# Prologue of a long-convolution kernel: position blocks loaded and multiplied half by half, decay read as a laid-out constant

## The chip, the cores and the metric

The kernel runs on one core of a Trainium2 chip. The metric is the device time of one execution in microseconds. Three executions of the kernel before gave 2279.33, 2279.97 and 2280.75 us; their median, 2279.97 us, is the time before. A further execution was profiled: it took 2278.88 us, of which the profile's span, from the first to the last instruction, covers 2277.1 us.

A core has a matrix engine (TensorE, PE in the profile; its weight loads are shown apart as PEld), a vector engine (VectorE, DVE), a scalar engine (ScalarE, ACT), a general engine (GpSimd, POOL) and an engine that mostly issues transfers (SyncE, SP). Each works through its own instructions in order. Transfers are issued from the queues of SP, ACT and POOL and run on 16 shared DMA engines. On-chip memory has 128 partitions; products of TensorE land in a separate accumulator memory, PSUM.

## The reference

All arrays are 32-bit floats. The first part is a convolution along the sequence whose filter is made by a small network and damped by an exponential window; the second part is a feed-forward layer on its result.

```python
# x, v: (4, 12544, 128); pos_emb: (12544, 64); w1: (64, 64); w2: (64, 128)
h_mlp = np.maximum(pos_emb @ w1, 0.0) @ w2
window = np.exp(-0.01 * np.arange(S))[:, None]
h_filt = h_mlp * window
u = x * v
Uf, Hf = np.fft.rfft(u, n=2 * S, axis=1), np.fft.rfft(h_filt, n=2 * S, axis=0)
y = np.fft.irfft(Uf * Hf[None], n=2 * S, axis=1)[:, :S, :]
x = (x * y).reshape(B * S, D)
# moe weights w1, w2, w3: (128, 768); w_out: (768, 128)
out = np.maximum(np.maximum(x @ w1, x @ w2), x @ w3) @ w_out
```

The window falls below what a 32-bit float can hold after 128 x 82 = 10496 positions, so only these 10496 rows of `pos_emb` are used.

## The kernel before, in words

A position is written as n x 128 + p, with a block number n below 82 (`NH`) and a place p below 128. The Fourier transform of the sequence is done as a first product over n with the table `f1` (or `f1h` for the filter), and a second product over p with tables that hold the rest. The work runs in stages: a prologue (to about 112 us in the profile), a stage that multiplies the spectra of the first batch and of the filter, and then the long part, in which the feed-forward products of one batch run beside the convolution of the next. The order of instructions on every engine is that of the code: it is written by hand, and no scheduler moves them. Only the waits between engines, and the tiles' buffers, are put in by the framework.

The change lies in the prologue, which does two things side by side.

The filter. `posT`, the 64 features by position, is loaded into `pos`, which borrows the memory of `specH`. The 82 blocks are split into two halves of 41 (`HH`): half h = 0 lies in partitions 0 to 63, half h = 1 in partitions 64 to 127. Each half comes in four pieces (`cuts`), 64 partitions each, issued in turn from SP and ACT (line 303). `mlp_in(i)` (line 334) multiplies 16 places p of both halves by `w1`: for every place and half, a matmul with 64 rows of contraction, 41 stationary columns (the blocks) and 64 moving columns. Its 32 matmuls go into one of two PSUM tiles, `pm0` and `pm1`, in turn. The output of half h for odd or even place r goes to partitions from 64 * (h ^ r), so both halves share a tile: partitions 0 to 40 and 64 to 104. `mlp_out(i)` (line 346) takes the positive part and multiplies it by the decay `winr` in one VectorE instruction for each r, over 105 partitions and 512 columns, and writes it to `hs`, which borrows the memory of `spec`. There are 8 such rounds. The 32-matmul blocks are counted as 64 in the profile, since each 32-bit matmul is recorded twice. After the last, the loop `for f in range(0, FO, 4)` (line 949) calls `quad` (line 899), 16 matmuls and a ScalarE copy each, with `f1h`.

The decay. `winr` must hold the window by block in partitions, with the places of each parity in falling order. The kernel before loads two pieces of `window` from HBM into `win`, turns them on TensorE (`window_turn`, line 317), copies them on ScalarE into `winT`, and turns them back with a permuted identity, `back` (`window_back`, line 324). The tiles `win`, `winT` and `back` are lent from the pool in which the data loads `ut` live. The partitions 41 to 63 of the `pm` tiles, which no matmul writes, are zeroed by two memsets of partitions 32 to 63 (line 291).

The data. The sequence is cut into units of 16 channels. `u_load` (line 362) issues two transfers per unit from SP, `u_mul` (line 372) multiplies `x` and `v` on VectorE, `turn2` (line 890) transposes two units on TensorE (8 transposes and a ScalarE copy), and `early(u)` (line 908) does a `quad` with the data, its result put partly aside. Units 0 to 3 go through this between the rounds of `mlp_in`. Ahead of it all `warm_up` (line 309) issues 25 rounds of products of zeros, of four matmul records each.

`some(n)` issues VectorE instructions that convert the feed-forward weights from 64-bit; it begins with the loop over `f`.

Of the kernel before, what the change touches and what calls it, by code (L numbers as in the profile page):

```python
# [10 lines left out]
FP32 = mybir.dt.float32  # L11
# [5 lines left out]
P = 128  # L17
# [9 lines left out]
NH = 82  # L27
HH = NH // 2
# [63 lines left out]
def kernel(  # L92
# [15 lines left out]
    nc = tc.nc  # L108
    NG, _, _, B, NB = x.shape
    FO, S = posT.shape  # L110
# [19 lines left out]
    f1h_d = nc.inline_tensor(f1h_t, name="f1h_const").ap()  # L130
# [2 lines left out]
    wq_d = nc.inline_tensor(wq_t, name="wq_const").ap()  # L133
    sign = np.where(np.arange(N1) < NK, 1, -1).astype(np.float32)[:, None]
    sign_d = nc.inline_tensor(sign.copy(), name="sign_const").ap()
    order = 127 - (2 * np.arange(64)[None, :] + np.arange(2)[:, None]).ravel()
    back_d = nc.inline_tensor(np.eye(P, dtype=np.float32)[:, order].copy(), name="back_const").ap()
    eye_d = nc.inline_tensor(np.eye(P, dtype=np.float32), name="eye_const").ap()

    w_sb = [None] + [const.tile([D, DFF], FP32, name=f"w_sb{i}") for i in (1, 2)]  # L140
# [59 lines left out]
    def scratch(name, bufs):  # L200
        return sml.tile([P, 2 * HF], I32, tag=name, name=name, bufs=bufs)[:]

    def load_raw(i, h, eng):
        r = scratch("raw", 2)
        if i < 3:
            src = (moe_w1, moe_w2, moe_w3)[i].bitcast(I32).rearrange("(g c) f -> c g f", c=GC)
            for c in range(GC):
                eng.dma_start(r[c * NG:(c + 1) * NG],
                                  src[c][:, h * 2 * HF:(h + 1) * 2 * HF])
        else:  # L210
            src = moe_w_out.bitcast(I32).rearrange("(c p) d -> p c d", p=P)
            eng.dma_start(r.rearrange("p (c d) -> p c d", c=NF // 2),
                              src[:, h * NF // 2:(h + 1) * NF // 2, :])
        return r

    def convert(r, i, h):
# [35 lines left out]
    inp = ctx.enter_context(tc.tile_pool(name="inp", bufs=3))  # L252
# [3 lines left out]
    eye = raw0.tile([P, P], FP32, name="eye")  # L256
# [7 lines left out]
    fps = mps.enter_context(tc.tile_pool(name="fps0", bufs=2, space=PSUM))  # L264
# [5 lines left out]
    posv = pos.rearrange("f (n p) -> f p n", p=P)  # L270
    hs = spec[0:64 + HH].rearrange("p k r d -> p (k r d)")[:, 0:FO * P].rearrange(
        "n (f r t) -> n f r t", r=2, t=64)
    w1_sb = sml.tile([P, FO], FP32, name="w1_sb")
    w2_in = sml.tile([P, D], FP32, name="w2_in")
    w2x = pin.tile([P, D], FP32, name="w2x")

    def lent(n, name):
        return inp.tile([P, 4, NB], FP32, tag="u0", name=name)[:].rearrange(
            "p g n -> p (g n)")[:, 0:n]

    win = lent(P, "win")[0:64 + HH]
    winT = lent(2 * (64 + HH), "winT").rearrange("p (r n) -> p r n", r=2)
    winr = sml.tile([64 + HH, 2, 64], FP32, name="winr")
    back = lent(P, "back").rearrange("p (r t) -> p r t", r=2)
    f1h = sml.tile([64 + HH, 2, 2 * N1], FP32, name="f1h")
    warm = sml.tile([P, 256], FP32, name="warm")
    nc.vector.memset(warm[:], 0.0)
    nc.vector.memset(win, 0.0)
    pms = [fps.tile([P, 1024], FP32, name=f"pm{i}", bufs=1) for i in range(2)]
    for pm in pms:  # L290
        nc.vector.memset(pm[32:64], 0.0)
    for h in range(2):
        nc.gpsimd.dma_start(
            win[64 * h:64 * h + HH],
            window[0, h * HH * P:(h + 1) * HH * P].rearrange("(n p) -> n p", p=P))
    nc.gpsimd.dma_start(eye[:], eye_d)
    nc.gpsimd.dma_start(back.rearrange("p r t -> p (r t)"), back_d)
    for h in range(2):
        (nc.scalar if h else nc.sync).dma_start(w1_sb[64 * h:64 * h + 64], w1[:, :])
    cuts = (0, 11, 21, 31, HH)  # L300
    for j, (lo_, hi_) in enumerate(zip(cuts, cuts[1:])):
        for h in range(2):
            (nc.scalar if (h + j) % 2 else nc.sync).dma_start(
                pos[64 * h:64 * h + 64, lo_ * P:hi_ * P],
                posT[:, (h * HH + lo_) * P:(h * HH + hi_) * P])
    for r in range(2):
        nc.scalar.copy(winT[:, r, 0:64], warm[:, 0:64])

    def warm_up(n):

        ps = fps.tile([P, 1024], FP32, tag="cv", name="pw")
        for _ in range(n):
            halves_mm(ps[:, 0:256], warm[:, 0:P], warm[:], True, True)

    pw = fps.tile([P, 1024], FP32, tag="cv", name="pw")

    def window_turn():
        nc.tensor.transpose(pw[:, 0:64 + HH], win, eye[0:64 + HH, 0:64 + HH])
        for r in range(2):
            for h in range(2):  # L320
                c = 64 * (h ^ r)
                nc.scalar.copy(winT[:, r, c:c + HH], pw[:, 64 * h:64 * h + HH])

    def window_back():
        for r in range(2):
            nc.tensor.matmul(pw[0:64 + HH, 512 + 64 * r:576 + 64 * r], winT[:, r], back[:, r],
                             start=(r == 0), stop=True, skip_group_check=True)
        nc.scalar.copy(winr[:].rearrange("n r t -> n (r t)"), pw[0:64 + HH, 512:512 + P])

    def w2_order():  # L330
        nc.scalar.copy(w2x[:].rearrange("f (c g) -> f c g", c=GC),
                       w2_in[:].rearrange("f (g c) -> f c g", c=GC))

    def mlp_in(i):

        ps = pms[i % 2]
        for q in range(8):
            for r in range(2):
                for h in range(2):
                    c = 64 * (h ^ r)  # L340
                    nc.tensor.matmul(
                        ps[c:c + HH, 512 * r + q * FO:512 * r + (q + 1) * FO],
                        posv[64 * h:64 * h + 64, P - 1 - 2 * (8 * i + q) - r, :],
                        w1_sb[64 * h:64 * h + 64], start=(q == 0), stop=True,
                        skip_group_check=True)
    def mlp_out(i):
        v = pms[i % 2][0:64 + HH].rearrange("n (r t f) -> n r f t", r=2, t=8)
        for r in range(2):
            nc.vector.scalar_tensor_tensor(
                out=hs[:, :, r, 8 * i:8 * i + 8], in0=v[:, r], scalar=0.0,  # L350
                in1=winr[:, r, None, 8 * i:8 * i + 8].to_broadcast([64 + HH, FO, 8]),
                op0=ALU.max, op1=ALU.mult)

    NU = NG
# [7 lines left out]
    def u_load(b, u):  # L362
        c, g0 = divmod(u, NG // 4)
        ts = []
        for src in (xr, vr):
            t = pools(b, u).tile([P, 4, NB], FP32, tag=f"u{len(ts)}", name="ut")
            nc.sync.dma_start(
                t[:], src[4 * g0:4 * g0 + 4, :, c, b, :].rearrange("g p n -> p g n"))
            ts.append(t)
        us[u] = ts  # L370
# [519 lines left out]
    def turn2(u):  # L890

        t = utp.tile([NB, 8, 2, 64], FP32, tag="uT", name="uT")
        ps = fps.tile([P, 1024], FP32, tag="cv", name="pst")
        for v in range(2):
            turn(u + v, ps[:, 512 * v:512 * v + 512])
        nc.scalar.copy(t[:], ps[0:NB, :].rearrange("n (s t r) -> n s r t", s=8, r=2))
        uts[u] = t
# [10 lines left out]
    def early(u):  # L908
        t, v = uts[u - u % 2], 4 * (u % 2)
        quad([t[:, v + i] for i in range(4)], (f1, f1), aside[u],  # L910
             spec[:, NS:, :, 4 * u:4 * u + 4])

    warm_up(22)
    window_turn()
    warm_up(3)
    nc.scalar.dma_start(f1q[:], f1_d)
    for u in range(4):
        u_load(0, u)
    raws.append(load_raw(*jobs[0], nc.sync))
    for u in range(4, 6):  # L920
        u_load(0, u)
    raws.append(load_raw(*jobs[1], nc.sync))
    for i in range(9):
        if i in (4, 7):
            turn2(2 * (i // 7))
            for u in range(6 + 2 * (i // 7), 8 + 2 * (i // 7)):
                u_load(0, u)
        if i in (5, 6):
            early(i - 5)
        if i < 8:  # L930
            mlp_in(i)
        if i >= 7:
            early(i - 5)
        if i == 0:
            window_back()
            nc.scalar.dma_start(f1h[:], f1h_d)
            nc.scalar.dma_start(w2_in[0:FO], w2[:, :])
            nc.scalar.dma_start(w2_in[FO:P], w2[:, :])
        else:
            mlp_out(i - 1)  # L940
        if i in (3, 5):
            for u in range(i - 3, i - 1):
                u_mul(u)
    for u in (0, 2):
        uts.pop(u)
# [2 lines left out]
    fps = fin.enter_context(tc.tile_pool(name="fps", bufs=4, space=PSUM))  # L948
    for f in range(0, FO, 4):
        quad([hs[:, f + i] for i in range(4)], (f1h[:, 0], f1h[:, 1]), specH[:, :, :, f:f + 4])  # L950
        u, k = divmod(f // 4, 4)
# [12 lines left out]
    for u in range(4, NU, 2):  # L964
        t = uts.pop(u)
# [201 lines left out]
    for n, (b, i) in enumerate(tiles[:LAST]):  # L1167
# [9 lines left out]
        for f in range(NF):  # L1177
# [9 lines left out]
            h = up((b, i), f)  # L1187
# [42 lines left out]
    for i in range(0, NT, 2):  # L1230
        h = {}
        X, Y = banks if i % 4 == 0 else banks[::-1]
        for j, (name, f) in enumerate(ORDER):
            n = int(name[1]) - 1
# [5 lines left out]
            if step > 2 and weights:  # L1240
                out, a1, a2 = weights.pop(0)
# [57 lines left out]
```

## Time and profile before

| what | value |
|---|---|
| median of three executions | 2279.97 us (2279.33 to 2280.75) |
| the profiled execution | 2278.88 us |
| its span | 2277.1 us |
| TensorE busy | 2257.1 us, 99% of the span |
| VectorE, ScalarE, GpSimd busy | 69%, 52%, 39% |
| first product of positions on TensorE | at 16.08 us |
| first `mlp_out` on VectorE | at 18.87 us |
| quads with `f1h` start | at 39.34 us |

A line of the page's fifth part, or of an answer about groups, gives the line of the kernel, engine, operation, what is written from what, the shape, and the count; then the busy time, the mean length of one in ns, and the idle time before. A line of a timeline gives start, duration, engine, line and operation, with equal neighbours merged (x4: four of them); the bracket names the idle time before it and what ended that. The chain that ended last is followed back from the last instruction of the span to what each step waited for. The answers by stretch give for each engine the busy time and the count of instructions, and at the end the granted clock of TensorE, the busy share of the transfer engines and GB/s.

### The profile page before, as it was taken

The page shows a single profiled execution, that of the slowest core. Times are in us where ns is not written, and L with a number is a line of the kernel's source. Part 1 is how long each engine was busy: PE and PEld are TensorE (multiplying, and loading weights), DVE is VectorE, ACT ScalarE, POOL GpSimd, SP SyncE. Part 2 cuts the span into 40 slices and gives each one's busy share as a digit, 9 for nine tenths or more (in the row PEclk, how much of TensorE's full clock was granted, in tenths as well). Part 3 has the DMA queues.
Part 4 walks back from the last instruction along what each step waited for, and adds up shares of the span by engine and source line. Part 5 has one row for each costly group of instructions (what it writes and reads, how often), then busy time and mean ns, then how long its engine had stood idle before and what let it go on. Part 6 is the DMA issues. An engine that isn't in the chain of part 4 may idle for free.

```text
span 2277.1 us, 68484 instructions
## 1 busy us (share of the span) xinstructions
PE 2257.1 (99%) x27855; PEld 1376.3 (60%) x27855; DVE 1560.9 (69%) x2854; ACT 1174.9 (52%) x2129; POOL 877.6 (39%) x1089
## 2 busy tenths in 40 slices
PE   9999999999999999999999999999999999999998
PEld 7899866655555556655555556655555546666665
DVE  5589967677777757667878756658878754544443
ACT  3688844466666534456666534456666522222222
POOL 1045433323333334323333333423333326666666
PEclk9999999999999999999999999999999999999999
DMA  8778989699989689889999789979999732222221
GB/s 193 179 242 278 297 186 182 135 221 246 243 221 242 165 176 183 163 189 246 245 237 239 194 166 181 166 182 252 235 235 240 197 81 56 56 71 64 60 56 22
DMA packets 473365, 411.03 MB, mean 181 GB/s; under 512 B 327993, under 2 KB 374522, under 8 KB 473050
## 3 DMA queue, kind: packets, MB, share of 16 engines
q1 hardware_dynamic: 446034, 329.50, 63.8%
q0 software_dynamic: 26224, 75.44, 11.1%
q8 instruction: 219, 3.59, 0.7%
q10 hardware_dynamic: 792, 1.72, 0.3%
q14 instruction: 96, 0.79, 0.1%
HBM read 262.84 MB, written 84.67 MB: 153 GB/s over the span
## 4 chain that ended last, share of the span: by engine, by line
PE 96%; DVE 1%; DMA 0%; issue 0%; ACT 0%; SPq 0%; POOL 0%; POOLq 0%; DVEq 0%; ACTq 0%
PE hps L156 44%; PE ops L156 19%; PE ops L817 6%; PE cps L426 5%; PE cps L156 4%; PE ps L156 4%; PE cps L487 3%; PE cps L497 3%; PE ps L165 3%; PE sps L1045 2%; PE gps L1027 2%; PE last L156 1%; PE pst L379 1%; DMA zd<-zs 0%; DVE spec L439 0%
## 5 line engine op out<-in xcount | busy, mean ns | idle before, releaser
L156 PE MATMUL hps<-gt,w_sb 128*64 128x392 f32 x6144 | 1150.7, 495 | 0.7 <-DVE gt L744 0.7
L754 ACT ACTIVATE hid<-hps 128x392 f32<-128x392 f32 x768 | 383.7, 500 | 701.9 <-PE hps L156 684.4
L156 PEld LDWEIGHTS hps<-gt,w_sb 128*64 128x64 f32 x6144 | 430.6, 137 | 422.3 <-issue 387.9
L757 DVE TENSOR_TENSOR hid<-hid,hps 128x392 f32<-128x392 f32 x768 | 428.3, 558 | 335.6 <-PE hps L156 322.5
L156 PE MATMUL ops<-hid,wo_sb 128*64 128x392 f32 x2304 | 479.9, 492 | 0.0
L539 POOL TENSOR_TENSOR cb<-cb,xs 128x512 f32<-128x512 f32 x135 | 174.0, 1289 | 463.6 <-DVE xs L536 341.8
L156 PEld LDWEIGHTS ops<-hid,wo_sb 128*64 128x64 f32 x2304 | 171.7, 137 | 207.6 <-issue 202.2
L512 DVE TENSOR_TENSOR cb<-cps,eo 128x512 f32<-128x512 f32 (+1 forms) x288 | 175.2, 650 | 72.8 <-ACT eo L509 72.7
L439 DVE TENSOR_TENSOR spec<-cps,high 128x360 f32<-128x360 f32 x188 | 141.1, 791 | 122.2 <-ACT high L435 122.2
L772 POOL DMA_DIRECT2D out_dram<-ot x96 | 75.2, 783 | 348.1 <-ACT ot L770 318.3
L527 ACT ACTIVATE xs<-cb 32x512 f32<-32x512 f32 x270 | 169.6, 628 | 20.6 <-DVE cb L512 11.6
L435 ACT COPY high<-cps 128x360 f32<-128x360 f32 x94 | 75.0, 798 | 180.1 <-PE cps L426 148.4
L528 ACT COPY xs<-cb 32x512 f32<-32x512 f32 x270 | 166.3, 616 | 3.2
L426 PEld LDWEIGHTS cps<-f1q,uT 98*64 98x64 f32 x3008 | 131.4, 138 | 29.1 <-issue 24.2
L543 DVE TENSOR_TENSOR xs<-cb 128x256 f32<-128x256 f32 x270 | 140.9, 566 | 9.4 <-POOL cb L539 9.2
L426 PE MATMUL cps<-f1q,uT 98*64 98x90 f32 x3008 | 135.8, 242 | 1.6 <-DVE uT L410 1.1
L395 POOL COPY planes<-ut 128x784 uint16<-128x784 uint16 x90 | 76.1, 846 | 152.6 <-DVE ut L374 148.3
L520 POOL DMA_DIRECT2D zd<-cb x135 | 92.5, 686 | 62.1 <-DVE cb L512 57.4
L156 PEld LDWEIGHTS cps<-f4p,even 90*64 90x64 f32 x1552 | 89.5, 138 | 35.0 <-issue 33.4
L841 POOL DMA_DIRECT2D out_dram<-o x128 | 77.4, 610 | 51.9 <-DVE o L834 49.7
L156 PE MATMUL cps<-f4p,zt 90*64 90x49 f32 x1552 | 96.3, 222 | 0.0
L156 PE MATMUL cps<-f4p,even 90*64 90x49 f32 x1552 | 95.0, 220 | 0.0
(146 smaller groups left out, 3149.1 us busy)
## 6 DMA issues: line engine op xcount, KB each, us to landing
ht<-hd SPq DMA_DIRECT2D x264, 256.0 KB, 6.7
wt<-wq_const SPq DMA_DIRECT2D x144, 256.0 KB, 6.2
zd<-cb POOLq DMA_DIRECT2D x135, 256.0 KB, 6.0
zt<-zd SPq DMA_DIRECT2D x384, 90.0 KB, 2.9
sq<-spec SPq DMA_DIRECT2D x264, 128.0 KB, 6.7
ut<-in_xr_dram SPq DMA_DIRECT2D x128, 196.0 KB, 3.9
ut<-in_vr_dram SPq DMA_DIRECT2D x128, 196.0 KB, 4.3
xT<-in_x_dram SPq DMA_DIRECT2D x256, 98.0 KB, 3.2
```

The lines of the kernel that those rows point to most:

```text
L156: nc.tensor.matmul(out[64 * h:64 * h + 64], lhsT[:, 64 * h:64 * h + 64], rhs, start=start, stop=stop, skip_group_check=True)
L426: nc.tensor.matmul(ps[64 * c:64 * c + 64, 256 * i + h * N1:256 * i + (h + 1) * N1], t[:, 2 * ((at + i) % 8) + h].rearrange("n r t -> n (r ...
L439: nc.vector.tensor_tensor(out=spec[:, :, a, at:at + n], in0=v[:, 1], in1=high, op=op)
L512: nc.vector.tensor_tensor(out=cb[:, a, lo:hi], in0=ps[:, lo:hi], in1=eo[:, lo:hi], op=op)
L520: nc.gpsimd.dma_start(zd[b][2 * z:2 * z + 2].rearrange("k c t a f -> (k c t) a f"), zss.pop(z))
L527: nc.scalar.mul(xs[at:at + 32], xt[at + 32:at + 64], -1.0)
L528: nc.scalar.copy(xs[at + 32:at + 64], xt[at:at + 32])
L539: nc.gpsimd.tensor_tensor(out=xts[g], in0=xts[g], in1=xs[:], op=ALU.add)
L543: nc.vector.tensor_tensor(out=ab[:, q], in0=y[:, 0], in1=y[:, 1], op=(ALU.subtract, ALU.add)[q])
L754: nc.scalar.activation(h[:], pa[:, 0:N], Relu)
L757: nc.vector.tensor_tensor(out=h[:], in0=h[:], in1=pb[:, 0:N], op=ALU.max)
L817: nc.tensor.matmul(ps[64 * c:64 * c + 64, 0:H2], w, rhs[:, H2 * c:H2 * c + H2], start=start, stop=True, skip_group_check=True)
```

## The change

The positions are loaded half by half: all four pieces of half 0 first, then those of half 1, the pieces of a half in turn from SP and ACT. `mlp_in` and `mlp_out` get the half as an argument: a round has 16 matmuls of one half, and two VectorE instructions, one per r, over the 41 partitions that this half wrote, which start at partition 0 for one r and at 64 for the other. There are 16 rounds, eight of half 0 and then eight of half 1, still with two PSUM tiles in turn. The products of units 0 to 3 and their turns lie between the rounds of half 1, except that `u_mul` of units 0 and 1 comes ahead of the last `mlp_out` of half 0.

The decay is worked out on the host as a constant in the layout of `winr` and loaded once from the GpSimd queue. `win`, `winT`, `back` and both turns are gone, and with them the loans from the data pool.

The unwritten partitions are now zeroed in `hs` itself: partitions 32 to 63, half of the columns on VectorE and half on GpSimd, once, before the products. `warm_up` has 15 rounds. `f1h` and `w2` are issued before the rounds.

```diff
-    order = 127 - (2 * np.arange(64)[None, :] + np.arange(2)[:, None]).ravel()
-    back_d = nc.inline_tensor(np.eye(P, dtype=np.float32)[:, order].copy(), name="back_const").ap()
+    decay = np.exp(-0.01 * np.arange(P * NH, dtype=np.float32)).reshape(2, HH, P)
+    winr_t = np.zeros((64 + HH, 2, 64), np.float32)
+    for h in range(2):
+        for r in range(2):
+            c = 64 * (h ^ r)
+            winr_t[c:c + HH, r] = decay[h][:, 127 - r::-2]
+    winr_d = nc.inline_tensor(winr_t, name="winr_const").ap()
...
-    nc.vector.memset(win, 0.0)
     pms = [fps.tile([P, 1024], FP32, name=f"pm{i}", bufs=1) for i in range(2)]
-    for pm in pms:
-        nc.vector.memset(pm[32:64], 0.0)
-    for h in range(2):
-        nc.gpsimd.dma_start(
-            win[64 * h:64 * h + HH],
-            window[0, h * HH * P:(h + 1) * HH * P].rearrange("(n p) -> n p", p=P))
+    nc.gpsimd.dma_start(winr[:], winr_d)
     nc.gpsimd.dma_start(eye[:], eye_d)
-    nc.gpsimd.dma_start(back.rearrange("p r t -> p (r t)"), back_d)
+    for eng, lo_, hi_ in ((nc.vector, 0, FO // 2), (nc.gpsimd, FO // 2, FO)):
+        eng.memset(hs[32:64, lo_:hi_], 0.0)
...
-    for j, (lo_, hi_) in enumerate(zip(cuts, cuts[1:])):
-        for h in range(2):
-            (nc.scalar if (h + j) % 2 else nc.sync).dma_start(
+    for h in range(2):
+        for j, (lo_, hi_) in enumerate(zip(cuts, cuts[1:])):
+            (nc.scalar if j % 2 else nc.sync).dma_start(
                 pos[64 * h:64 * h + 64, lo_ * P:hi_ * P],
                 posT[:, (h * HH + lo_) * P:(h * HH + hi_) * P])
-    for r in range(2):
-        nc.scalar.copy(winT[:, r, 0:64], warm[:, 0:64])
...
-    def mlp_in(i):
+    def mlp_in(h, i):
         ps = pms[i % 2]
         for q in range(8):
             for r in range(2):
-                for h in range(2):
-                    c = 64 * (h ^ r)
-                    nc.tensor.matmul(
...
+                c = 64 * (h ^ r)
+                nc.tensor.matmul(
...
-    def mlp_out(i):
-        v = pms[i % 2][0:64 + HH].rearrange("n (r t f) -> n r f t", r=2, t=8)
+    def mlp_out(h, i):
         for r in range(2):
+            c = 64 * (h ^ r)
+            v = pms[i % 2][c:c + HH].rearrange("n (r t f) -> n r f t", r=2, t=8)
             nc.vector.scalar_tensor_tensor(
-                out=hs[:, :, r, 8 * i:8 * i + 8], in0=v[:, r], scalar=0.0,
-                in1=winr[:, r, None, 8 * i:8 * i + 8].to_broadcast([64 + HH, FO, 8]),
+                out=hs[c:c + HH, :, r, 8 * i:8 * i + 8], in0=v[:, r], scalar=0.0,
+                in1=winr[c:c + HH, r, None, 8 * i:8 * i + 8].to_broadcast([HH, FO, 8]),
                 op0=ALU.max, op1=ALU.mult)
...
-    warm_up(22)
-    window_turn()
-    warm_up(3)
+    warm_up(15)
     nc.scalar.dma_start(f1q[:], f1_d)
     for u in range(4):
         u_load(0, u)
+    nc.scalar.dma_start(f1h[:], f1h_d)
+    nc.scalar.dma_start(w2_in[0:FO], w2[:, :])
+    nc.scalar.dma_start(w2_in[FO:P], w2[:, :])
...
-    for i in range(9):
-        if i in (4, 7):
-            turn2(2 * (i // 7))
-            for u in range(6 + 2 * (i // 7), 8 + 2 * (i // 7)):
-                u_load(0, u)
-        if i in (5, 6):
-            early(i - 5)
-        if i < 8:
-            mlp_in(i)
-        if i >= 7:
-            early(i - 5)
-        if i == 0:
-            window_back()
...
-        else:
-            mlp_out(i - 1)
-        if i in (3, 5):
-            for u in range(i - 3, i - 1):
+    for n in range(17):
+        if n in (9, 12):
+            u = 2 * (n // 12)
+            turn2(u)
+            for v in range(u + 6, u + 8):
+                u_load(0, v)
+        if n in (10, 11, 13, 14):
+            early(n - 10 - n // 13)
+        if n < 16:
+            mlp_in(*divmod(n, 8))
+        if n:
+            mlp_out(*divmod(n - 1, 8))
+        if n in (7, 10):
+            for u in range(2 * (n // 10), 2 * (n // 10) + 2):
                 u_mul(u)
```

## The prediction

> **What bounds the kernel now.** I read the page first: how much of the span TensorE works, and which engine the chain that ended last runs through.
>
> ```profile
> PE 2257.1 (99%) x27855; PEld 1376.3 (60%) x27855; DVE 1560.9 (69%) x2854; ACT 1174.9 (52%) x2129; POOL 877.6 (39%) x1089
> ...
> PE 96%; DVE 1%; DMA 0%; issue 0%; ACT 0%; SPq 0%; POOL 0%; POOLq 0%; DVEq 0%; ACTq 0%
> ```
>
> The chain is TensorE for 96% of the span. What the prologue saves or loses before the point where TensorE stays full therefore arrives at the end one to one. That point comes from the chain in order of time, asked for the first 62 us:
>
> ```profile
> 39.30 0.04 issue
> 39.34 3.94 PE ps L165 x96
> 43.28 1.01 PE pst L379 x8
> 44.29 5.11 PE ps L165 x128
> ```
>
> At 39.34 the products of `hs` with `f1h` begin (the loop of `quad` calls over `f`). From there TensorE goes on without pauses apart from 0.97 us at 59.86 and 1.3 us near 112. The question is at what time those quads start after the change. The timeline before them (start, duration, engine, line, what; in brackets the idle time ahead):
>
> ```profile
> 16.08 1.93 PE L341 MATMUL pm<-w_sb,specH 64*41 64x64 f32 x64 [1.61 <-issue]
> ...
> 18.87 2.82 DVE L349 SCALAR_TENSOR_TENSOR spec<-pm,winr 105x512 f32<-105x512 f32 x4 [15.40 <-ACT winr L328]
> ...
> 23.23 1.05 DVE L374 TENSOR_TENSOR ut<-ut 128x392 f32<-128x392 f32 x2
> 24.21 1.08 PE L379 MATMUL pst<-eye,ut 128*98 128x128 f32 x8
> ...
> 35.86 1.29 DVE L349 SCALAR_TENSOR_TENSOR spec<-pm,winr 105x512 f32<-105x512 f32 x2 [1.42 <-PE pm L341]
> ...
> 39.34 3.94 PE L165 MATMUL ps<-f1h,spec 105*64 105x90 f32 x96 [0.92 <-ACT spec L174]
> ```
>
> TensorE waits until 16.05 (its first weight load) for all positions, is held up by the turned decay (VectorE starts at 18.87), and from 24.21 on is full: it, not VectorE, sets the pace, and the last wait is for ScalarE's copy of the fourth early quad. VectorE is idle for much of 25 to 36. Transfers:
>
> ```profile
> 0.00:5.00 5.00, 3.81 (x18) 2.19 (x20) 2.24 (x4) 0.91 (x1) 2.57 (x8) 1.00 0.47 107
> 5.00:10.00 5.00, 5.00 (x48) 3.23 (x46) 0.00 (x0) 0.77 (x3) 0.00 (x0) 1.00 1.05 219
> ```
>
> The last two columns (DMA share, GB/s) say that the loads are limited by the transfer engines.
>
> [...]
>
> **The change, part by part.**
>
> Start of TensorE. Half of the positions is 64 rows x 5248 x 4 B = 1.34 MB; with `w1`, `winr` and `eye` 1.50 MB. The two rows above give 1.63 MB by 10.0 us, so 1.50 MB at 9.4. The packet records agree: the first four pieces of before ended at 9.79, the last at 14.97, and TensorE started 1.08 us after that. So 9.8 + 1.1 = 10.9 (10.4 to 11.9) in place of 16.05. The 15 warm-up rounds are done near 9.7.
>
> Decay. Transpose, two products (0.58), seven copies on ScalarE, three Pool loads and TensorE's 0.5 us at 17.94 go; one load of 54 KB comes, on the Pool queue, which nothing blocks. It is needed at 12; the window pieces landed 5.8 us after issue. Worth: VectorE no longer waits until 18.87.
>
> Zeroing. Two memsets of `pm` (0.91 each) become one of 32x4096 on VectorE and one on Pool. [...] Pool: 256 elements copied in 0.40, so about 6.4, done near 9. [...]
>
> TensorE's blocks. 8 blocks of 32 matmuls become 16 of 16. A 32-matmul block took 1.68 us (28.29 to 29.96), 64 records, 26 ns each, alternating row groups. Now one row group streams: at the quads' 90 columns per 41 ns, 64 columns take 29 ns, 0.93 us a block. Low end 0.84 (26 ns); high end 1.05.
>
> VectorE's blocks. 16 instructions of 105x512 become 32 of 41x512; columns set the time, so each still lasts 0.69. Before, a pair took 1.29, i.e. the second started 0.61 after the first. Now outputs start at partitions 0 and 64 in turn, each is held, and I take 0.69 plus a hand-over of 0.03 (dependent conversions at 38.83 and 39.22, of 0.35, leave 0.04): 0.72. Low end 0.61 (no hold); high end 0.86 (two memsets at 1.48 and 2.56, of 0.91, left 0.17). VectorE's total thus goes from 11 to 23 us: more than doubled, in an engine that had slack, but now queued in front of the `u_mul`s that TensorE's turns need.
>
> Queues. `u_load`s move ahead of the decay: the first is issued near 9 instead of 13.06, but their semaphores are shared with the position loads, so unit 1's are issued at about 16 to 17 (14.1 to 16.2 before). `f1h` and `w2` move from 18.6 to ahead of 16 on ACT's queue, behind all positions. After 15.0, 0.36 MB (ACT) and 0.80 MB (units 0, 1) at 255 KB/us land by 19.6 plus 1 = 20.6; needed at 22.0. Units 2 and 3, 3.1 us later, 23.7; needed at 27.4. Hidden, by 1.4 and 3.7 us.
>
> The sum, block by block with two `pm` buffers. First product on VectorE at 10.9 + 0.93 + 0.12 = 11.95. Seven pairs of 1.44 end at 22.03; two `u_mul`s of 0.52 at 23.07. Turn 23.03 to 24.04. VectorE's eighth pair ends 24.51 and frees `pm1`, so block 9 runs 24.58 to 25.51. Then TensorE: early quad (1.39) to 26.90, block to 27.83, quad to 29.22, block to 30.15, turn (1.01) to 31.16, block to 32.09, wait for ScalarE's copy to 32.38, quad to 33.77, block to 34.70, quad to 36.09, two blocks to 37.95. VectorE's last two pairs, 37.14 to 40.02, end it. Quads start at 40.09, against 39.34: +0.75 us. The profiled execution took 2278.88 (span 2277.1 and 1.8 around it), so 2279.6; the median lies 1.09 above that execution: 2280.7.
>
> **Rivals.**
>
> No hold: pairs of 1.22. Then quads start at 38.04, -1.3 us, 2278.7; with 26 ns matmuls and transfers 0.5 us earlier, 37.1, 2277.7. For it: the pairs before do overlap. [...]
>
> A larger hold or a cold clock: 0.86 per instruction gives 42.9, +3.6 us, 2283.5. TensorE works only 0.93 of each 1.44 us at first, and after a window in which it was busy 1.87 of 3.40 us the trace shows half clock:
>
> ```profile
> 298.60:302.00 3.40, 1.87 (x48) 1.57 (x46) 1.99 (x3) 1.49 (x2) 0.00 (x0) 1.00 0.83 208
> 302.00:305.40 3.40, 2.74 (x22) 1.36 (x20) 1.36 (x3) 0.37 (x1) 1.74 (x2) 0.50 0.36 107
> ```
>
> Blocks of 1.8 us in place of 1.44 for 6.8 us would add 1.4 us.
>
> Slower: weight loads not hidden within one row group. [...] It passes 0.2% from blocks of about 1.43 us. Against it: the 41 ns of the quads.
>
> The whole promise kept: VectorE never waits after 11.95 at 0.61 and 0.48, ending at 33.4, -5.9 us, 2274.1. Against: TensorE's chain from the first turn alone needs 14 us.
>
> **How the numbers follow.** 0.2% is 4.6 us, about what a measurement can tell from no change. Forecast (hold of 0.69 to 0.75; -0.4 to +1.7 us) 0.50; no hold 0.25; large hold or cold clock 0.15; weight loads 0.07; promise kept 0.03. Range: 2277.5 (no hold, fast matmuls) to 2285.0 (0.86 and slow matmuls 4.3 us, and 0.7); the likeliest's own 2279.5 to 2282.5. Faster: the last case and a little of no hold, 0.04; slower: weight loads and a quarter of the third, 0.11; within, 0.85.
>
> **What would show it.** First block near 10.9; pairs of instructions with starts 0.72 apart; block starts to ends 0.93; first turn near 23; quads at 40.1. Wrong if starts are 0.61 apart (faster), if blocks exceed 1.43, if units 0 and 1 land after 22, or if the half clock shows before 40 us.

## The result

The changed kernel takes 2298.59 us (median of six executions, 2295.97 to 2301.76) against 2280.08 us for the kernel before beside it: a ratio of 1.0083 (95% interval 1.0070 to 1.0096). It is slower by 18.5 us. The forecast was 2280.7 us with a range to 2285.0, so it was wrong.

The profiled execution of the changed kernel took 2300.47 us. From its page, the busy times, the granted clock by slice, and the chain that ended last:

```profile
span 2298.7 us, 68391 instructions
...
PE 2275.8 (99%) x27810; PEld 1395.3 (61%) x27810; DVE 1574.2 (68%) x2868; ACT 1173.4 (51%) x2122; POOL 881.1 (38%) x1088
...
PEclk6999999999999999999999999999999999999999
...
PE 96%; DMA 1%; DVE 1%; issue 0%; ACT 0%; SPq 0%; POOL 0%; POOLq 0%; DVEq 0%; ACTq 0%
```

TensorE is still the bound: its busy time has grown by 18.7 us, while the profiled span is 21.6 us longer (2298.7 against 2277.1). The clock line shows one low slice, the first. The answer by stretch (busy time and count of PE, PEld, DVE, ACT and POOL, then clock, DMA share, GB/s) puts edges on it:

```profile
10.00:13.50 3.50, 1.75 (x32) 1.33 (x29) 0.00 (x0) 0.00 (x0) 0.00 (x0) 1.00 1.05 220
13.50:20.00 6.50, 6.50 (x124) 6.43 (x123) 4.82 (x7) 1.28 (x1) 0.00 (x0) 0.50 1.11 233
20.00:30.00 10.00, 10.00 (x162) 9.45 (x159) 8.65 (x14) 0.09 (x1) 0.00 (x0) 0.50 0.97 228
...
50.00:61.00 11.00, 9.31 (x142) 8.91 (x140) 7.44 (x18) 2.02 (x4) 0.62 (x1) 0.50 0.01 1
61.00:70.00 9.00, 9.00 (x190) 8.42 (x188) 8.55 (x23) 5.57 (x7) 3.77 (x8) 0.98 0.69 177
```

The kernel before, in the middle of the same part:

```profile
20.00:30.00 10.00, 9.53 (x308) 8.76 (x302) 7.38 (x13) 1.88 (x3) 0.00 (x0) 1.00 0.92 228
```

TensorE of the changed kernel ran at half clock from 13.5 us, 1.2 us after its first product of positions, to 61.3 us. The mean clock of all six executions is 0.987 to 0.989 (before: 0.998 in the profiled one), so this happened in each of them. The chain in order of time shows what it did:

```profile
2.26 9.94 DMA specH<-in_pos_emb_dram
...
12.33 15.66 PE pm L315 x288
27.99 1.88 PE pst L355 x8
29.87 1.89 PE pm L315 x32
31.76 2.60 PE ps L170 x32
...
51.58 3.62 PE pm L315 x64
...
56.86 5.14 PE ps L170 x72
```

The first nine blocks of products (288 records, 32 each) took 15.66 us, 1.74 a block; the forecast had 0.93 for TensorE, and VectorE's 1.44 as the pace. A turn took 1.88 in place of 1.01, an early quad 2.60 in place of 1.39. The quads with `f1h` start at 56.86, where the kernel before had 39.34 and the forecast 40.09. Against the forecast that is 16.77 us, which add up like this:

- First block 1.43 later (12.33 against 10.9).
- From there to the first turn 15.66 against 12.13: 3.5.
- Two turns 1.7 and four early quads 4.8 longer.
- Seven more blocks together 6.6 longer; the waits that the forecast had between them, and one at the end, shrink by 1.3. From first turn to quads this makes 11.8.

After the start the quads still run at half clock until 61.3, which costs 2.1 us more (the first 96 records take 6.07 us, before 3.94). The long part of the kernel begins 20.8 us later than before (324.17 against 303.41); the 1.1 us that this adds were not traced.

The timeline of the changed kernel shows VectorE and the memsets:

```profile
2.04 3.47 DVE L289 MEMSET spec<- 32x4096 f32 x1 [0.91 <-issue]
2.62 3.50 POOL L289 MEMSET spec<- 32x4096 f32 x1
...
17.67 1.39 DVE L325 SCALAR_TENSOR_TENSOR spec<-pm,winr 41x512 f32<-41x512 f32 x2 [0.33 <-PE pm L315]
...
27.09 2.69 DVE L325 SCALAR_TENSOR_TENSOR spec<-pm,winr 41x512 f32<-41x512 f32 x4
...
56.86 6.07 PE L170 MATMUL ps<-f1h,spec 105*64 105x90 f32 x96 [1.69 <-DVE spec L325]
```

VectorE waits 0.33 us for TensorE ahead of each pair: it was not the bound. A pair lasts 1.39 in place of 1.29: where the partition changes, an instruction (0.68 to 0.70 long) starts when the one before has ended, so the hold is there. In the four neighbours at 27.09 the starts are 0.70, 0.62 and 0.70 apart; the short one lies between two instructions that begin at the same partition.

### The profile page after: what moved, and what is told of

The parts are those of the page before. It is cut to its first block, busy times and chain, and to the rows that moved or that the text cites. A ratio compares the mean times of both kernels' runs of the same rounds, so it can differ in the third digit from the quotient of the medians.

```text
span 2298.7 us, 68391 instructions
## 1 busy us (share of the span) xinstructions
PE 2275.8 (99%) x27810; PEld 1395.3 (61%) x27810; DVE 1574.2 (68%) x2868; ACT 1173.4 (51%) x2122; POOL 881.1 (38%) x1088
## 3 DMA queue, kind: packets, MB, share of 16 engines
q0 software_dynamic: 26160, 75.38, 10.9%
## 4 chain that ended last, share of the span: by engine, by line
PE 96%; DMA 1%; DVE 1%; issue 0%; ACT 0%; SPq 0%; POOL 0%; POOLq 0%; DVEq 0%; ACTq 0%
PE hps L161 44%; PE ops L161 19%; PE ops L793 6%; PE cps L402 5%; PE cps L161 4%; PE ps L161 3%; PE ps L170 3%; PE cps L463 3%; PE cps L473 3%; PE sps L1016 2%; PE gps L998 2%; PE pm L315 1%; PE last L161 1%; PE pst L355 1%; DMA specH<-in_pos_emb_dram 0%; DMA wt<-wq_const 0%
```

## The experiments

Three questions: is it the order of the products, the clock, or one of the other edits? "Before" is the kernel before, timed on the same chip beside each run. All times are medians; ratios have 95% intervals.

### Was it the pause ahead of the first block?

TensorE stood still for 1.75 us ahead of its first block, at 10.58 to 12.33. More warm-up fills that.

```diff
-    warm_up(15)
+    warm_up(22)
```

> The changed kernel with 22 warm-up rounds in place of 15, so that TensorE works without a pause up to the first block of positions (the pause was 1.75 us at 10.58). Pause theory (the pause alone let the clock fall, and it stayed down): the clock stays full, blocks of 16 matmuls take 0.93 us, the quads with f1h start near 42, the time is 2282 to 2284 us. Row-group theory (blocks that use one row group of 64 partitions count as too little activity, whatever stands before them): the half clock comes within 7 us after the first block, blocks take 1.7 us, the quads start at 56 to 58, the time is 2297 to 2301 us.

Measured: 2298.93 us, ratio 1.0084 (1.0067 to 1.0101), mean clock 0.988 to 0.989 in its four executions. From its answer by stretch:

```profile
10.00:13.50 3.50, 3.50 (x47) 2.44 (x44) 0.00 (x0) 0.00 (x0) 0.00 (x0) 1.00 1.04 215
...
20.00:30.00 10.00, 9.53 (x159) 9.30 (x159) 7.67 (x12) 0.00 (x0) 0.00 (x0) 0.50 0.95 228
```

No pause was left, the clock still halved, at 18.1 us in place of 13.5, and came back at 62.5, and the quads started at 57.93. The pause can have hastened the halving, but it was not the cause of the loss.

### The order of products alone

The kernel before, with the 16 products of one half ahead of the 16 of the other in each round. Loads, sizes, decay and VectorE's instructions are those of before.

```diff
-        for q in range(8):
-            for r in range(2):
-                for h in range(2):
+        for h in range(2):
+            for q in range(8):
+                for r in range(2):
```

> The kernel before with one thing changed: within each round of 32 matmuls the 16 of half 0 come first and then the 16 of half 1, so that one row group of 64 partitions is used at a time; loads, waits and VectorE's instructions are those of before. Pause theory: no change, full clock, quads at 39.3, 2280 us (within 1 us). Row-group theory: the half clock comes within 10 us after 16.1, rounds take 3.4 us in place of 1.7, the quads start at 48 to 55, the time is 2289 to 2296 us.

Measured: 2295.8 us, ratio 1.0059 (1.0037 to 1.0081). Its six executions fall in two groups: 2285.2 and 2286.6 with a mean clock of 0.998 to 0.999, and 2295.8 to 2301.0 with 0.988 to 0.990. The profiled one is of the first group. Its timeline:

```profile
32.23 2.94 PE L341 MATMUL pm<-w_sb,specH 64*41 64x64 f32 x64
...
35.10 1.46 PE L165 MATMUL ps<-f1q,uT 98*64 98x90 f32 x32
...
46.88 3.32 PE L165 MATMUL ps<-f1h,spec 105*64 105x90 f32 x80 [0.92 <-ACT spec L174]
```

A round of the kernel before, from its timeline:

```profile
28.29 1.74 PE L341 MATMUL pm<-w_sb,specH 64*41 64x64 f32 x64
29.96 1.46 PE L165 MATMUL ps<-f1q,uT 98*64 98x90 f32 x32
```

With one half after the other a round runs from 32.23 to 35.10: 2.87 us for 64 records, 45 ns each on average, against 26 before (28.29 to 29.96), at full clock. The records of one half alone lie 48 ns apart; around the change from one half to the other they are closer. The quads start 7.5 us later. So there are two effects, and the order alone brings both: at full clock the products of one half are slower, and in four executions of six some 10 us more go with the lower clock.

### The other edits alone

The kernel before with `winr` as a constant (both turns and the loans gone, 25 rounds of warm-up); and that with the loads of half 0 first as well.

```diff
-    for j, (lo_, hi_) in enumerate(zip(cuts, cuts[1:])):
-        for h in range(2):
-            (nc.scalar if (h + j) % 2 else nc.sync).dma_start(
+    for h in range(2):
+        for j, (lo_, hi_) in enumerate(zip(cuts, cuts[1:])):
+            (nc.scalar if j % 2 else nc.sync).dma_start(
```

> The kernel before with the decay part alone: winr loaded as a constant, no turns, no loan from the data pool; loads and rounds of positions as before, 25 warm-up rounds. Both theories: full clock throughout. TensorE loses the 0.5 us of the turn back and VectorE starts at 17.9 in place of 18.9, so the first turn of the data comes at 23.3 in place of 24.2 and the quads start at 38.4: 2279.1 us, 0.9 below before.

> The kernel before with the constant decay and the changed kernel's order of position loads (all of half 0, then half 1), but rounds of both halves with alternating row groups. Load theory (the order of loads costs transfer time or brings the clock down): positions complete later than 16.3, 2282 us or more. Tile-height theory: the order of loads is harmless, 2278 to 2280 us as with the constant decay alone; rounds of 1.7 us.

Measured: constant decay 2278.23 us, ratio 0.9991 (0.9982 to 0.9999); with the loads reordered 2278.85 us, 0.9996 (0.9987 to 1.0005). Neither edit costs anything that these runs show. The interval of the constant decay lies just below 1, but its profile shows no gain in this part: the quads start at 39.24, not at the expected 38.4. Its clock did not stay full either: it was half for 3.4 us from 17.7, and in the other form from 17.9, after TensorE had waited about 3 us for the positions.

### Which alternation matters?

Two forms of the kernel before. In the first, all four places (two halves of the rows by two output column groups) stay in use, in another order. In the second only the diagonal two do: the two halves of the rows (the row groups) still alternate from one product to the next, but each has one column group. (Half of the products then land in other partitions, so other numbers come out.)

```diff
-            for r in range(2):
+            for c2 in range(2):
                 for h in range(2):
-                    c = 64 * (h ^ r)
+                    r = h ^ c2
+                    c = 64 * c2
```

> The kernel before with the order of the four matmuls of a place pair changed so that neighbours differ in the row group and share the column group in each pair (before: the first two pairs differ in both). Tile-height theory: alternating row groups is enough, rounds of 1.7 us, full clock, 2280 us. If it takes a change of both groups, rounds lie between 2 and 2.9 us and the time is 2283 to 2296 us.

```diff
-                    c = 64 * (h ^ r)
+                    c = 64 * h
```

> The kernel before with one edit: the output column group is 64 * h in place of 64 * (h ^ r), so only two of the four 64x64 positions are used, on the diagonal, but the row groups still alternate from one matmul to the next. Two of the four sets of products land in the other partitions, so the first block of the output is not the reference's. Theory tile positions: 48 to 52 ns a matmul, rounds of 32 take 2.9 to 3.3 us in place of 1.68, quads start 6 to 10 us later than 39.3, 2286 to 2292 (more if the clock drops). Theory strided weights or weight loads within one row group: 26 ns, 1.68 to 1.75 us, 2279 to 2281.

Measured: four places in another order 2279.51 us, 0.9996 (0.9988 to 1.0005), the quads at 39.71. Two places on the diagonal 2284.41 us, 1.0018 (1.0011 to 1.0025). The timeline of the latter:

```profile
34.90 2.54 PE L341 MATMUL pm<-w_sb,specH 64*41 64x64 f32 x64
...
37.38 1.08 PE L379 MATMUL pst<-eye,ut 128*98 128x128 f32 x8
...
44.47 3.94 PE L165 MATMUL ps<-f1h,spec 105*64 105x90 f32 x96 [0.92 <-ACT spec L174]
```

A round takes 2.48 us, 39 ns a record: between the two theories, so neither holds as it was put. Alternating row groups don't restore the 26 ns. Its clock stayed at 0.997 or more in all 20 executions.

### Both halves of the rows in every product

If the height of the tile were what matters, products over all 128 rows would help: the weights of both halves are read, and `w1` for the other half is zero, so the results stay the same. First the kernel before with the order of the second experiment, then the changed kernel (here the first block waits for all positions, since all 128 rows are read, and the warm-up has 25 rounds).

```diff
-                    posv[64 * h:64 * h + 64, P - 1 - 2 * (8 * i + q) - r, :],
-                    w1_sb[64 * h:64 * h + 64], start=(q == 0), stop=True,
+                    posv[:, P - 1 - 2 * (8 * i + q) - r, :],
+                    w1_sb[:, h], start=(q == 0), stop=True,
```

> As the kernel before with half 0 ahead of half 1 in each round, but each matmul uses all 128 partitions: the weights of w1 are laid out with zeros in the other half's rows, so that the products are the same. Tile-height theory (blocks of one 64-partition row group cannot hide their weight loads and leave the clock unguarded; a full-height tile can): 26 to 30 ns per record, rounds of 1.7 to 1.9 us, full clock, quads at 39.3 to 40.5, 2280 to 2282 us. Order theory (taking one half after the other is what costs, whatever the tile): rounds of 2.9 us and 2285 to 2300 us as with 64-partition tiles.

> The changed kernel with full-height matmuls (w1 laid out with zeros in the other half's rows), 25 warm-up rounds; since each matmul now reads both halves, the first block waits for all positions as in the kernel before. Tile-height theory: full clock, blocks of 0.9 to 1.0 us, VectorE sets the pace at 0.70 us an instruction, the quads start at 44.5 to 46, 2285 to 2287 us, that is 12 us below the changed kernel although its first block is 4 us later. Split theory (half-size blocks and twice as many VectorE instructions are what costs): 2296 us or more.

Measured: 2290.26 us, 1.0049 (1.0034 to 1.0064), and 2292.09 us, 1.0060 (1.0045 to 1.0075). Both were slower than expected. The changed kernel in this form:

```profile
36.67 1.67 PE L316 MATMUL pm<-w_sb,specH 128*41 128x64 f32 x32
...
38.15 1.44 PE L170 MATMUL ps<-f1q,uT 98*64 98x90 f32 x32
...
52.38 3.94 PE L170 MATMUL ps<-f1h,spec 105*64 105x90 f32 x96 [1.74 <-DVE spec L326]
```

The quads are back at 1.44 us: the mean clock is 0.997 or more in all eight executions of the two, and in the profiled ones only one stretch of 3.4 us before 23 us is at half clock. That stretch is not due to the height: the forms with the constant decay above, with four places, have it too. But a block still takes 1.48 us (36.67 to 38.15), and 1.62 where blocks follow each other. Full height keeps the clock and does not quicken the products. So the two effects come apart, and the theory of the height of the tile fell for the first.

### Filler between the blocks

The changed kernel with two products of zeros, over all rows, behind each of the eight blocks of half 0.

```diff
+        if n < 8:
+            halves_mm(fill[:, 0:256], warm[:, 0:P], warm[:], True, True)
```

> The changed kernel with two full-height products of zeros (four records of 109 ns at full clock, 0.44 us) behind each of the eight blocks of half 0, in the time in which TensorE waits for VectorE. Their results are not used. The pause ahead of the first block stays. Pause theory: the half clock starts at the pause as in the changed kernel, the added products cost 0.9 us per round at half clock, quads at 60 or later, 2300 us or more. Row-group theory: the added products hold the clock up while half 0 is multiplied; VectorE sets the pace at 1.39 us a pair, the quads start at 42 if the clock also holds through half 1, which has its own full-height products, and the time is 2282 to 2284 us; if it falls there, 2287 to 2292 us.

Measured: 2305.09 us, 1.0102 (1.0074 to 1.0130). One execution of four kept the clock up to the quads (2293.26 us, mean 0.998; in the stretch from 50 to 61 us it is 0.84); the others took 2304.3 to 2307.8 at 0.986 to 0.987. The profiled one is that of full clock:

```profile
14.18 1.74 PE L315 MATMUL pm<-w_sb,specH 64*41 64x64 f32 x32
15.84 0.65 PE L161 MATMUL pw<-warm 128*64 128x256 f32 x4
```

At full clock a block of the changed kernel takes 1.66 us (14.18 to 15.84). The filler kept the clock once in four times. That execution was 5 us faster than the changed kernel; the others were 6 to 9 us slower.

### The stride of the weights

The quads, whose 41 ns the forecast had taken as its measure, read 64 neighbouring weights. The products of positions read 41 weights 128 elements apart: `posv[..., p, :]` takes every 128th column. Here other columns are read, 41 neighbours, so other numbers come out; count, order and tile positions stay, and each block still needs all pieces of its half.

```diff
-                    posv[64 * h:64 * h + 64, P - 1 - 2 * (8 * i + q) - r, :],
+                    pos[64 * h:64 * h + 64, HH * (8 * (15 - 2 * q - r) + i):HH * (8 * (15 - 2 * q - r) + i + 1)],
```

> The changed kernel with one edit: the weights (the stationary operand) of each product of mlp_in are 41 neighbouring columns of the positions in place of every 128th column (a stride of 512 bytes). Other columns are multiplied, so the first block of the output is not the reference's; count, tile positions, sizes and order stay. Each block still needs all four pieces of its half. Theory strided weights (loading 41 weights at a stride is what takes about 48 ns, one row group loads one set at a time, two row groups load side by side): the 64 columns then take 64/1.14/2 = 28 ns a matmul as the quads' 90 take 41 on two column groups, a block 0.9 to 1.0 us, the quads start at 39 to 42, full clock; 2279 to 2283. Theory tile positions (each of the array's four 64x64 positions is held about 100 ns by one load and one product whatever the addresses, and one half of the positions uses two of the four): block 1.66 to 1.72, quads at 52 to 57, 2290 to 2302. Theory half clock from the short pauses as the main cause: the clock drops near 13.5 all the same, quads above 52.

> The kernel before with the weights of mlp_in taken from neighbouring columns as in e9 (other columns are multiplied: the first block of the output is not the reference's). Theory strided weights: with four positions the 64 columns take 64/1.14/4 = 14 to 20 ns a matmul, rounds of 32 take 0.9 to 1.3 us in place of 1.68, the quads start 1.5 to 4 us earlier, 2276 to 2279. Theory tile positions whatever the addresses, or weight loads within one row group: 26 ns, 1.68 us, quads at 39.3, 2279.5 to 2281.

Measured in the kernel before: 2277.17 us, 0.9991 (0.9983 to 0.9998), quads at 38.47. Its timeline:

```profile
26.37 1.10 PE L341 MATMUL pm<-w_sb,specH 64*41 64x64 f32 x64
...
27.41 1.46 PE L165 MATMUL ps<-f1q,uT 98*64 98x90 f32 x32
```

A round takes 1.04 us in place of 1.68: 16 ns a record. The stride is the cost of these products in the kernel before too. The quads moved up by 0.9 us only, since TensorE then waits for other engines.

In the changed kernel: 2297.52 us, 1.0073 (1.0058 to 1.0088). The answer by stretch for the instructions on `pm` alone (PE, PEld and DVE, then the clock):

```profile
12.50:13.50 1.00, 1.00 (x38) 1.00 (x40) 0.00 (x0) 1.00 0.98 194
14.00:15.00 1.00, 0.92 (x18) 0.69 (x16) 0.95 (x3) 0.50 1.09 216
```

(A count takes in the products under way when its stretch begins.) While the clock was full, the records' starts lay 28 ns apart on average. At 13.5 us it halved, as in the changed kernel, and the pace became 52 ns; the quads started at 56.17 and nothing was gained. With neighbouring weights the half clock by itself gives blocks of 1.72 us; with a stride, full clock gives 1.66. Either cause suffices for the blocks.

### Both causes taken away, and the clock by itself

First the full-height form of the changed kernel with neighbouring weights: full clock, no stride, everything else as in the change, but 25 rounds of warm-up and the first block late again. Then the changed kernel with neighbouring weights and 22 rounds of warm-up: no stride and no pause, but one half of the rows.

```diff
-                    posv[:, P - 1 - 2 * (8 * i + q) - r, :],
+                    pos[:, HH * (8 * (15 - 2 * q - r) + i):HH * (8 * (15 - 2 * q - r) + i + 1)],
```

> The kernel of the full-height form of the change (e8) with neighbouring weights as in e9: two tile positions, full height, full clock expected as there, and only the stride of the weights differs from e8 (the first block of the output is not the reference's). Strided weights as a cause of their own: a block of 16 takes 0.87 to 0.95 us in place of 1.55 to 1.67, VectorE's held pairs of 1.40 to 1.44 become the pace of the first eight, and the quads start at 46 to 47.5 in place of 52.4; 2285.5 to 2287.5 (e8: 2292.1). If the number of tile positions alone sets the 52 ns at full clock: blocks of 1.55 to 1.67 and quads at 52.4 as in e8, 2291 to 2293.

> e9 with 22 warm-up rounds in place of 15, so that TensorE has no pause ahead of the first block, and at full clock its records are 27 ns apart. Half clock from products in half of the array's rows alone, whatever their density: the clock halves within 7 us of the first block although nothing paused, quads at 54 to 58, 2295 to 2299. Half clock from the pause and from thin streams (strided weights): the clock stays full, blocks of 0.9 us, quads at 41 to 42.5, 2280.5 to 2283.

Measured: the first 2287.65 us, 1.0035 (1.0023 to 1.0048), against 2292.09 with the stride. Its timeline:

```profile
26.51 1.09 PE L316 MATMUL pm<-w_sb,specH 128*41 128x64 f32 x32 [0.33 <-DVE spec L326]
27.93 1.09 PE L316 MATMUL pm<-w_sb,specH 128*41 128x64 f32 x32 [0.33 <-DVE spec L326]
...
34.02 1.07 PE L316 MATMUL pm<-w_sb,specH 128*41 128x64 f32 x32
...
34.91 1.41 PE L170 MATMUL ps<-f1q,uT 98*64 98x90 f32 x32
...
47.02 3.94 PE L170 MATMUL ps<-f1h,spec 105*64 105x90 f32 x96 [2.30 <-DVE spec L326]
```

Now TensorE waits for VectorE, blocks follow its held pairs 1.42 us apart, and a block that nothing holds up takes 0.89 us (34.02 to 34.91). A few records run ahead while the last positions land; the unbroken row of blocks starts at 17.82, and the quads follow 29.20 us later. The forecast had 29.19 from first block to quads. With both causes gone (but for 3.4 us at half clock from 18.6), the kernel does what the forecast said, 6.9 us late. That the two agree to 0.01 us is chance: the half clock cost something at the start, and the waits are not the forecast's (the last is 2.30 us, where it had 2.14).

The second: 2298.31 us, 1.0082 (1.0066 to 1.0097). Its stretches:

```profile
10.00:13.50 3.50, 3.50 (x40) 2.13 (x38) 0.00 (x0) 0.00 (x0) 0.00 (x0) 1.00 1.04 224
13.50:20.00 6.50, 4.34 (x135) 3.72 (x129) 5.39 (x8) 1.28 (x1) 0.00 (x0) 0.98 1.09 219
20.00:30.00 10.00, 9.89 (x160) 9.69 (x161) 7.59 (x13) 0.00 (x0) 0.00 (x0) 0.50 1.03 232
```

Nothing paused ahead of the blocks, the records were 28 ns apart at first (0.90 us a block), and the clock halved at 19.8 us all the same, until 60.7; the quads started at 57.28. Here TensorE waits for VectorE, 0.33 us ahead of some blocks; the full-height kernel above waits just as long for it, and got its clock back after 3.4 us. What differs is the rows in use, and with them the work done in the same time, to which the last section comes back.

## Why the prediction was wrong

**The step that failed is "TensorE's blocks".** It priced a block by the quads: "at the quads' 90 columns per 41 ns, 64 columns take 29 ns, 0.93 us a block". Two things that the quads don't share were left out.

- The stride. The quads read neighbouring weights, the blocks read every 128th. Without the stride the step's number is right: 0.89 us measured with full height, 0.90 in one half of the rows. With it, at full clock, 1.66 us. The kernel before hid this, since its 26 ns came from four places at once. Records by weights and places, all at full clock: strided, four places 26 ns; two on the diagonal 39; two within one row group 45 in the rounds of the second experiment, which change the half midway, and 52 in the blocks of the changed kernel (1.66 us by 32). Neighbouring: four places 16; two within one row group 28. With the stride, going from four places to two costs 13 ns, and leaving the alternation of row groups another 6 to 13. Where in the read the stride costs was not measured.
- The clock. The forecast knew the half clock from the stretch at 302 us and allowed it 6.8 us of time and 1.4 us of cost, after a pause. It lasted 47.8 us and needed no pause: with the pause filled the clock halved at 18.1 us.

**The size of each.** Without the clock, the changed kernel's quads would start near 47.8: the full-clock execution with filler had them at 52.48, less eight fillers of 0.59. That is an estimate, 8.5 us after the 39.34 of before, or 7.7 more than forecast; 1.1 of that is its first block (11.96 against 10.9), and some 6.6 are the strided blocks. The half clock brings the rest, 56.86 less 47.8, or 9 us, and 2 more until 61.3. The two are not a plain sum. With the stride gone and the clock still half the time falls by 1 us only (2297.52); with the clock kept and the stride left, by 6.5 with a first block 5.6 us late (2292.09).

**The slower rival**, "weight loads not hidden within one row group", had the right place and sign: it was to pass 0.2% from blocks of 1.43 us, and the blocks took 1.74. It got 0.07, for the 41 ns of the quads (96 records in 3.94 us). Its mechanism is not what the runs show, since 28 ns within one row group with neighbouring weights is as fast as the quads in proportion to the columns. But the conclusion from those 41 ns, that blocks in one row group run at the quads' rate, was wrong, and the kernel's own code showed how they differ.

**"A larger hold or a cold clock"** named the clock, but took a pause as its trigger. The records show TensorE 100% busy from 13.5 to 50 us at half clock, so busy time is not what counts here; the work done in it fits better (last section).

**Start of TensorE.** Forecast 10.9 (10.4 to 11.9), measured 12.33. The rate was as forecast: the two stretches of 5 us to 10.0 have 113 and 213 GB/s, 1.63 MB, as before. But the pieces of half 1 were issued from 2.63 on, while half 0 was still on its way, so not all of that can have been half 0's; the step took all of it as such, and was off by 1.4 us.

**Decay and zeroing.** Right, but for the memset on Pool, which took about half of its estimate. The memset on VectorE took 3.47 us (1024 elements took 0.91 before, so four times that is 3.6), that on Pool 3.50 (forecast about 6.4); both were done by 6.2, far ahead of the first product. The constant decay costs nothing; a gain of its own is at most 0.2% and not shown in the profile.

**VectorE's blocks.** Right: the hold, which the profile of the kernel before does not show in this part, is in that of the changed kernel, with starts 0.70 apart where the partition changes (0.72 forecast) and 0.62 where it doesn't. In the changed kernel it was hidden behind TensorE; with both causes gone it set the pace, at 1.42 us a pair.

**Queues.** Right as far as it showed: `u_mul` of units 0 and 1 began at 26.01, directly behind a `mlp_out`, and waited for no transfer. Loading one half first cost no rate by itself (113 and 213 GB/s in the two stretches to 10.0, before 107 and 219).

**One to one to the end.** Right: quads 17.5 us later, 2.1 more until the clock returned, 20.8 at the start of the long part, and 21.6 more in the span.

## What to carry to other kernels

Here the rate of one matmul did not price another whose weights are read at another stride, nor one with fewer places of the array in use: with strided weights a record cost 26 ns with four places and 45 to 52 in one half of the rows, where 28 were possible with neighbouring weights. Compare the stride and the places before a rate is carried over. Before splitting a stage so that it begins with half of its partitions, ask what else the full width did: here it kept four places of the array in use, and with them enough work to hold the clock (156 rows x columns per ns in a round, against 79 in a block of one half). When a rival would cost far more than what is at stake, one look at the address pattern of both sides is worth more than one number against it.

## What was not expected of the hardware

- Long runs of products in one half of the rows went with half clock, without a pause and with records 28 ns apart as with 52: in all 18 executions of the changed kernel and its three variants with such blocks and no filler (clock 0.987 to 0.990). With the halves in turn by 16 products it was four in six; with full-height filler, three in four; with two places in both row groups, none in 20; with full-height products, half of whose weights meet zeros, none in 14 (0.996 or more).
- The kept traces show what the lost clock goes with. In all fifteen profiles the granted clock changes only after 3.41 us or a multiple of it (the changed kernel: 6.83, 47.79, 262.83 and 3.41 us; the kernel before: 296.96 and 6.83). For each step I added up rows times moving columns of the matmul records that start in it, and divided by its length. (A block of the changed kernel at full clock, 32 records of 64 rows and 64 columns in 1.66 us, does 79 per ns; a round of the kernel before, 64 of them in 1.68 us, 156.) In the first 66 us, from the first record of the clock on, this work in one step goes with the clock of the next, with one exception (91, followed by half):

| clock in a step | work in it, rows x columns per ns | clock in the next step |
|---|---|---|
| full | 12 to 77, and once 91 | half (10 steps) |
| full | 88 or more | full (190 steps) |
| half | up to 102 | half (49 steps) |
| half | 122 or more | full (10 steps) |

Neither busy time nor rows alone separate these steps. Two of them, first from the kernel with the long warm-up, then from that of the second experiment, for the instructions on `pm`:

```profile
14.67:18.08 3.41, 3.36 (x70) 3.22 (x68) 3.10 (x5) 1.00 1.07 219
...
20.56:23.97 3.41, 3.41 (x97) 3.41 (x96) 1.85 (x3) 1.00 1.07 269
```

In both TensorE is busy with products of 64 rows only. The first, with 64 records that start in it (77 per ns), was followed by half clock, the second, with 89 (107), by full; the counts shown take in those under way at the start. By this account products in one half of the rows lost the clock because, read at a stride or held up by VectorE, they did too little work per step. This is read from the traces after the fact, and no experiment of its own tried it. It is not the whole rule either: near 300 us four steps with 93 to 124 at full clock were followed by half clock. Whether the weight columns count as well was not separated.

- The half clock went on for as long as the work per step stayed in the table's third row. At half clock blocks in one half of the rows do at most 77 per ns, and steps with turns and early quads between them at most 102. The clock came back after the first step that quads with `f1h` filled, 57.9 to 61.3 us, with 127. Products with four places or full height do 144 to 152 at half clock, and there it came back after one step of 3.4 us. In the account the filler counts although it multiplies zeros: in its full-clock execution the steps with it have 100 to 131.
- At half clock a block with neighbouring weights took 1.72 us, about twice its 0.89; with strided weights it took 1.72 as well, against 1.66 at full clock. The cost of the stride nearly vanishes when the clock is half.
